# Token order of the key tiles, values in four loads, and scores by pairs of heads at the start of a fused attention and feed-forward kernel

## The chip, the cores and the metric

The kernel runs on one core of a Trainium2 chip. The metric is the device time of one execution in microseconds. Six parts of the core matter here: PE multiplies matrices, ACT evaluates functions, DVE and POOL work on vectors, SP issues stores, and 16 DMA engines move data. Loads that also convert from 32-bit to 16-bit floats are issued by POOL.

## The reference

```python
# q, k, v: (8, 12, 448, 64); w_in (768, 2048); w_out (2048, 768); beta (2048)
scores = q @ k.T / sqrt(64) - log(448)          # per batch and head
x = sigmoid(scores) @ v                         # 12 heads side by side: (8 * 448, 768)
h = x @ w_in
g = h * sigmoid(beta * h)
out = g @ w_out                                 # (3584, 768), float32
```

The sum over keys runs over all 448 of them, so the order in which keys stand inside a tile is free as long as k and v have the same one.

## The kernel before, in words

All matrix work is in 16-bit floats with sums in 32 bits. Everything is written in one order by hand (`tc.manual_schedule()`), and each engine does its instructions in that order; waits come only from data and from buffers.

**Heads and groups.** Four heads make a group (`g`, 24 in all, 3 for each batch), and two heads of a group make a slot. `load_one` (line 122) loads q or k of a group so that a partition holds one of 32 blocks of 14 tokens of one head (four heads times 32). `transpose` (line 201) turns blocks of 32 x 32 on DVE and leaves q and k with the head dimension on partitions: a head has 32 partitions, and its 64 dimensions are two passes (`e`). For k it needs two DVE instructions: one for the three full key tiles of 128 tokens (L217), one for the last 64 tokens (L221).

**Key tiles and values.** The 14 tokens of a block are numbered c. Before, quarter i of the 128 partitions of key tile j holds token c = 3i + j, and the last, half-filled tile holds c = 12 and 13. `load_v_full` (line 143) loads the values of the full tiles in four DMAs, `load_v_last` (line 155) those of the last tile in two. `double_v_last` (line 168) copies the last tile's 64 partitions to the other 64, on DVE, since two slots share one score tile there.

**Scores and weights.** `score` (line 231) issues one matmul (L237) that uses 32 of the 128 rows of the array. In the first batch the 448 queries are done in two halves of 224: `half_visit(g, c0, second)` (line 300) takes key tiles 0 and 1 of both slots (`second` = 0) or tile 2 and the last (`second` = 1), fills two score tiles with 16 matmuls that go through all four heads in turn, and then calls `weigh` (line 248) for each tile: one ACT sigmoid from PSUM to `attns` (L250, 896 or 448 columns). When only two score tiles are left, one sigmoid does both (L265, 1792 columns). `attend` (line 322) multiplies by the values (L340), and DVE casts the result to `xT` (L349). Score tiles are pairs of PSUM banks that are used in turn: three at first, two after the entry `("two",)`.

**First dense layer.** `dense1` (line 355) multiplies `xT` by `w_in` (L362), six matmuls for a block of 128 hidden columns; a sigmoid on ACT (L374) and a product on DVE (L377) give `gt`. In the first batch blocks 0 to 7 are done for the first half of the queries as soon as it is there. A "dense" unit in the list is one such matmul. Later the second layer (L392, L651) follows, largely by Strassen's scheme, and stores go out through SP.

**Order of the start.** `LOADS` (line 784) is the order of POOL's first DMAs after two that SP issues (k of group 0, and the first half of its q): q and k of groups 1 and 2, values of batch 0, the other halves of q, then eight loads of `w_in` with two blocks of 128 columns each. `LATER` (line 789) follows: group 3, `w_out`, the values of batch 1, and so on. `BEGIN` (line 838) is the order of the compute up to the first regular visit: casts, transposes, scores, idle matmuls on a tile of zeros (L822), values, dense units. In it `("q", 1, 0)` stands ahead of `("k", 1)`.

**Afterwards** each visit computes the scores of one key tile of a group, and a pace (`MORE`, line 900, moves single units between visits; `LATE` delays values) fills dense units between visits. There are 74 visits. From batch 1 on `load_v` loads a whole batch, and `double_v_last` copies it at a fixed visit.

Of the kernel before, what the change touches and what calls it, by code (L numbers as in the profile page):

```python
# [13 lines left out]
def kernel(  # L14
# [10 lines left out]
    nc = tc.nc  # L25
# [10 lines left out]
    PAIR = D // BLK  # L36
    JF = S // P
    KL = S - JF * P
    NF = JF * P // BLK
    NPAIR = H // 2  # L40
    QPB = H // HQ
    NHC = DM // P
# [97 lines left out]
    def last_base(s: int) -> int:  # L140
        return (s % 2 ^ swapped(s // 2)) * KL

    def load_v_full(b: int, lo: int = 0, hi: int = H):

        if b not in vs:
            vs[b] = vp.tile([P, H, JF + 1, D], FP16, tag="v16", name="v16")
        rows = v[b, lo:hi].rearrange("h (p c) d -> p h (c d)", c=NB)
        for i in range(HQ):
            nc.gpsimd.dma_start(
                out=vs[b][i * BLK : (i + 1) * BLK, lo:hi, 0:JF].rearrange("p h j d -> p h (j d)"),  # L150
                in_=rows[:, :, JF * i * D : JF * (i + 1) * D],
            )
            ready.update((b, "full", t, i) for t in range(lo // HQ, hi // HQ))

    def load_v_last(b: int):
        if b not in vs:
            vs[b] = vp.tile([P, H, JF + 1, D], FP16, tag="v16", name="v16")
        rows = v[b].rearrange("h (p c) d -> p h c d", c=NB)
        for c in range(NF, NB):
            lo = (c - NF) * BLK  # L160
            nc.gpsimd.dma_start(out=vs[b][lo : lo + BLK, :, JF], in_=rows[:, :, c])
        ready.add((b, "last"))

    def load_v(b: int):
        load_v_full(b)
        load_v_last(b)

    def double_v_last(b: int):
        assert (b, "last") in ready
        ready.add((b, "v"))  # L170
        nc.vector.tensor_copy(out=vs[b][KL:P, :, JF], in_=vs[b][0:KL, :, JF])

    WOUT = 2

# [26 lines left out]
    def transpose(g: int, r: int, c0: int = 0, c1: int = NB):  # L201
        raw = raws[g][:, r]
        assert g or (r, c0) == (0, NB // 2) or all((r, "cast", c) in ready for c in range(c0, c1))
        if r == 0:
            if g not in qT:
                qT[g] = qTp.tile([P, NB * BLK, PAIR], FP16, tag="qT", name="qT")
            ready.update((g, "q", c) for c in range(c0, c1, NB // 2))
            nc.vector.transpose(
                out=in_order(g // QPB, qT[g][:, c0 * BLK : c1 * BLK]),
                in_=raw[:, c0:c1].rearrange("p c d -> p (c d)").bitcast(FP32),  # L210
            )
            return
# [4 lines left out]
        nc.vector.transpose(  # L217
            out=to[:, 0 : JF * P].rearrange("p (j i q) -> p i j q", j=JF, i=HQ),
            in_=frm[:, 0:NF].rearrange("p (i j) f -> p i j f", j=JF),
        )  # L220
        nc.vector.transpose(  # L221
            out=to[:, JF * P :], in_=frm[:, NF:].rearrange("p c f -> p (c f)")
        )

    def score_tile():
        i, j = scored[n_sc[0] % len(scored)]
# [73 lines left out]
    def half_visit(g: int, c0: int, second: int):  # L300
# [18 lines left out]
        for s, jt, sco, u0 in plan:  # L319
            at_use(ats[id(sco)], (s, jt, c0), slice(u0, u0 + QH))  # L320

    def attend(g: int, c0: int, n: int, part=(0, 1)):
# [3 lines left out]
        assert (b, "v") in ready and (b, "full", t, HQ - 1) in ready  # L326
# [438 lines left out]
    with tc.manual_schedule():  # L765
        def load(what, *a):
            if what == "q":
                load_one(a[0], 0, a[1] * NH, (a[1] + 1) * NH)
            elif what == "k":
                load_one(a[0], 1)  # L770
            elif what == "qk":
                load_qk(a[0])
            elif what == "v":
                load_v_full(0, a[0] * HQ, a[1] * HQ)
            elif what == "last":
                load_v_last(0)
# [12 lines left out]
        LATER = [  # L789
# [42 lines left out]
        def beta_columns():  # L832
# [16 lines left out]
        for what, *a in BEGIN:  # L849
            if what == "q":  # L850
# [1 line left out]
                transpose(g, 0, half * NH, (half + 1) * NH)  # L852
            elif what == "k":
                transpose(a[0], 1)
            elif what == "scores":
                half_visit(a[0], a[1] * QH, a[2])
            elif what == "cast":
                cast(*a)
            elif what == "idle":
                idle_units(a[0])  # L860
            elif what == "v":
                double_v_last(a[0])
# [32 lines left out]
        def left_us(n: int):  # L895
# [2 lines left out]
        AV_US = 1.5  # L898
        GLANCE = 3
        MORE = {  # L900
# [3 lines left out]
        }  # L904
        RESERVE = (1.99, 3.28)
        LATE = {
# [122 lines left out]
```

## Time and profile before

| what | value |
|---|---|
| runs shown | 373.19, 373.23, 375.86 us; median 373.23 |
| profiled execution | 374.6 us, its span 372.8 us |
| PE busy | 365.8 us (98%), 2906 matmuls |
| DVE, ACT, POOL busy | 254.5, 259.9, 90.6 us |
| granted PE clock | 1.00 |
| matmuls L651 and L531 | 27% and 26% of the chain that ended last |
| sigmoid of 896 columns (L250), mean of one between 4 and 31 us | 1008 ns |
| issue of a value load, of a w_in load on POOL | 615 ns, 871 ns |

A line of the timeline has the start in us, the busy time of the merged instructions, the engine, the line of the code, what it writes and reads, the size, and how many; in brackets stands the engine's idle time before it and what ended that. A line of the stages has the stretch, its length, and for each engine the busy time and the number of instructions, then the granted PE clock, the DMA engines' share (over 1 where packets overlap) and their rate.

### The profile page before, as it was taken

The page shows a single profiled execution, that of the slowest core. Times are in us where ns is not written, and L with a number is a line of the kernel's source. Part 1 is how long each engine was busy: PE and PEld are TensorE (multiplying, and loading weights), DVE is VectorE, ACT ScalarE, POOL GpSimd, SP SyncE. Part 2 cuts the span into 40 slices and gives each one's busy share as a digit, 9 for nine tenths or more (in the row PEclk, how much of TensorE's full clock was granted, in tenths as well). Part 3 has the DMA queues.
Part 4 walks back from the last instruction along what each step waited for, and adds up shares of the span by engine and source line. Part 5 has one row for each costly group of instructions (what it writes and reads, how often), then busy time and mean ns, then how long its engine had stood idle before and what let it go on. Part 6 is the DMA issues. An engine that isn't in the chain of part 4 may idle for free.

```text
span 372.8 us, 7320 instructions
## 1 busy us (share of the span) xinstructions
PE 365.8 (98%) x2906; PEld 184.4 (49%) x2906; DVE 254.5 (68%) x479; ACT 259.9 (70%) x311; POOL 90.6 (24%) x136
## 2 busy tenths in 40 slices
PE   7989999999999999999999999999999999999997
PEld 4566644443444455544444445554444455555655
DVE  3435696877496966787667666778667666669671
ACT  5995777699876658887777749887787647883000
POOL 6833253151151012325123003235100002230000
PEclk9999999999999999999999999999999999999999
DMA  9999999993359030039829511018903111000334
GB/s 162 165 189 202 197 203 201 245 125 51 49 76 183 2 86 1 0 51 125 157 42 206 108 26 33 3 17 116 172 6 86 42 44 42 1 2 1 86 84 128
DMA packets 42626, 34.65 MB, mean 93 GB/s; under 512 B 21968, under 2 KB 39008, under 8 KB 42592
## 3 DMA queue, kind: packets, MB, share of 16 engines
q0 software_dynamic: 36688, 22.47, 44.5%
q1 hardware_dynamic: 5904, 11.71, 11.1%
q8 instruction: 23, 0.38, 0.4%
q14 instruction: 11, 0.09, 0.1%
HBM read 45.62 MB, written 11.01 MB: 152 GB/s over the span
## 4 chain that ended last, share of the span: by engine, by line
PE 92%; ACT 5%; issue 1%; DMA 1%; DVE 1%; ACTq 0%
PE ps L651 27%; PE ps L531 26%; PE ps L237 11%; PE ps L340 10%; PE ps L362 9%; PE ps L392 4%; PE ps L445 4%; ACT attns L250 3%; DMA gt<-in_k_dram 1%; ACT attns L265 1%; ACT sg L374 1%; DVE gt L377 0%; DVE kT L217 0%; ACT raw L806 0%; ACT osb L672 0%
## 5 line engine op out<-in xcount | busy, mean ns | idle before, releaser
L265 ACT ACTIVATE attns<-ps,nlogs 128x1792 f16<-128x1792 f32 x75 | 131.6, 1755 | 41.7 <-PE ps L237 41.6
L651 PEld LDWEIGHTS <-sum 128*128 128x128 f16 x440 | 40.5, 98 | 37.3 <-issue 12.5
L545 POOL TENSOR_TENSOR gt<-attns,sg 128x448 f16<-128x448 f32 x21 | 23.9, 1139 | 141.7 <-ACT sg L542 141.7
L237 PE MATMUL ps<-qT,kT 32*128 32x448 f16 (+3 forms) x864 | 52.1, 339 | 1.2 <-ACT attns L250 0.4
L542 ACT ACTIVATE sg<-ps,beta_sb 128x448 f32<-128x448 f32 x72 | 45.2, 632 | 8.4 <-PE ps L531 5.9
L531 PE MATMUL ps<-xT,w_in 128*128 128x448 f16 x216 | 49.2, 353 | 0.0
L531 PE MATMUL ps<-xT,w_S 128*128 128x448 f16 x216 | 49.2, 352 | 0.0
L651 PE MATMUL ps<-w_T,sum 128*128 128x384 f16 x264 | 48.7, 327 | 0.0
L545 DVE TENSOR_TENSOR gt<-ps,sg 128x448 f16<-128x448 f32 x72 | 44.3, 618 | 4.0 <-ACT sg L542 3.8
L349 DVE CAST xT<-ps 128x448 f16<-128x448 f32 (+1 forms) x54 | 28.8, 567 | 21.0 <-PE ps L340 21.0
L531 PEld LDWEIGHTS <-w_in 128*128 128x128 f16 x288 | 28.0, 98 | 26.6 <-issue 0.7
L362 PE MATMUL ps<-xT,w_in 128*128 128x448 f16 (+1 forms) x240 | 39.9, 316 | 1.2 <-DMA w_in<-in_moe_w_in_dram 0.6
L340 PE MATMUL ps<-attns,v 128*64 128x448 f16 (+3 forms) x432 | 40.4, 340 | 0.6 <-issue 0.6
L669 DVE TENSOR_TENSOR osb<-ps,osb 128x384 f32<-128x384 f32 x55 | 30.5, 554 | 15.1 <-PE ps L651 12.8
L638 DVE TENSOR_TENSOR sum<-gt 128x1024 f16<-128x1024 f16 x55 | 36.5, 678 | 0.2
L377 DVE TENSOR_TENSOR gt<-ps,sg 128x448 f16<-128x448 f32 (+1 forms) x40 | 20.1, 527 | 23.2 <-ACT sg L374 23.1
L126 POOL DMA_DIRECT2D raw<-in_q_dram x26 | 14.5, 559 | 79.6 <-DVE kT L221 72.6
L651 PE MATMUL ps<-w_out,gt 128*128 128x384 f16 x176 | 33.3, 327 | 0.0
L651 PE MATMUL ps<-w_out,sum 128*128 128x384 f16 x176 | 32.3, 327 | 0.0
L591 DVE TENSOR_TENSOR ps<-ps,attns 128x448 f32<-128x448 f32 x24 | 15.2, 632 | 23.3 <-PE ps L531 19.3
L362 PEld LDWEIGHTS <-w_in 128*128 128x128 f16 x240 | 21.8, 98 | 18.0 <-issue 5.4
L531 PEld LDWEIGHTS <-w_S 128*128 128x128 f16 x216 | 21.1, 98 | 19.4
(54 smaller groups left out, 376.4 us busy)
## 6 DMA issues: line engine op xcount, KB each, us to landing
out_dram<-osb SPq DMA_DIRECT2D x100, 96.0 KB, 2.1
raw<-in_k_dram POOLq DMA_DIRECT2D x23, 224.0 KB, 5.5
raw<-in_q_dram POOLq DMA_DIRECT2D x21, 224.0 KB, 3.9
v<-in_v_dram POOLq DMA_DIRECT2D x32, 144.0 KB, 6.2
w_in<-in_moe_w_in_dram POOLq DMA_DIRECT2D x8, 384.0 KB, 11.8
w_out<-in_moe_w_out_dram POOLq DMA_DIRECT2D x4, 768.0 KB, 13.4
v<-in_v_dram POOLq DMA_DIRECT2D x16, 48.0 KB, 6.1
out_dram<-osb SPq DMA_DIRECT2D x5, 144.0 KB, 2.4
```

Of the source, the lines that this page charges most:

```text
L237: nc.tensor.matmul(sco[base : base + nk, hh, u0 : u0 + n], kT[g][lo : lo + BLK, jt * P : jt * P + nk, e], qT[g][lo : lo + BLK, c0 : c0 + n ...
L265: nc.scalar.activation(out=attns[:, slot : slot + 2].rearrange("p n h s -> p (n h) s"), in_=sco, func=AF.Sigmoid, bias=nlogs[:, 0:1], scal ...
L340: nc.tensor.matmul(av[hh * D : (hh + 1) * D, 0:n], vs[b][base : base + nk, 2 * (s % NPAIR) + hh, jt], at[base : base + nk, hh, 0:n], start ...
L349: nc.vector.tensor_copy(out=xTs[b][:, s % NPAIR, c0 : c0 + n], in_=av[:, 0:n])
L362: nc.tensor.matmul(m1, w_in16[:, hc, dc * P : (dc + 1) * P], xTs[b][:, hc, c0 : c0 + n], start=(hc == 0), stop=(hc == NHC - 1),)
L377: nc.vector.tensor_tensor(out=gt[:, dc, off : off + n], in0=m1, in1=sg[:, 0:n], op=ALU.mult)
L531: nc.tensor.matmul(out, w[:, c, i * P : (i + 1) * P], m[:, c], start=(start and c == 0), stop=(c == KH - 1), skip_group_check=not start,)
L542: nc.scalar.activation(out=sg, in_=h, func=AF.Sigmoid, bias=0.0, scale=beta_sb[:, dc : dc + 1])
L545: return lambda: engine.tensor_tensor(out=gt[:, dc, b % 2 * S : b % 2 * S + S], in0=h, in1=sg, op=ALU.mult)
L638: nc.vector.tensor_tensor(out=sums[t, i], in0=x, in1=y, op=op)
L651: nc.tensor.matmul(m2, (x if op is None else sums[t, i])[:, dc], w[:, dc], start=first, stop=(dc == ND - 1), skip_group_check=i >= 4,)
L669: nc.vector.tensor_tensor(out=out, in0=in0, in1=in1, op=op)
```

## The change

Five things change; the arithmetic does not.

1. Token order: quarter i of the partitions now holds 4, 4, 3, 3 consecutive tokens (`rows_of`: first token 0, 4, 8, 11), the jth of them in key tile j. So the last tile's tokens are 3 and 7, and come with the others. The values of a batch are four DMAs with runs of 4 or 3 tokens of one head. In batch 0 they are loaded in two parts: heads 0 to 3 (group 0) first, heads 4 to 11 later, with four DMAs each.
2. The two DVE transposes of k are now halves of 256 and 192 columns (quarters 0 and 1, quarters 2 and 3) in place of 384 and 64.
3. The copy of the last value tile is done for batch 0 in the same two parts.
4. `pair_visit` replaces the half visits with `second` = 0 while three score tiles are in use: it takes one slot, that is two heads, and both key tiles 0 and 1, into one score tile with 8 matmuls, and its sigmoid follows.
5. Other orders: group 1's k ahead of its q, and group 0's values ahead of group 2's q, in the loads; group 0's values between group 1's scores in `BEGIN`; 29 idle matmuls for 42; 18 and 12 dense units around the scores of group 2 for 21 and 9, 33 for 39 before the third group's transposes; `MORE` changes at visits 2 and 3 by one unit each, and names 80 and 82 too.

```diff
+    def rows_of(i: int):
+        n = JF + int(i < KL // BLK)
+        return i * JF + min(i, KL // BLK), n
...
+    def load_v(b: int, lo: int = 0, hi: int = H):
...
         for i in range(HQ):
+            c, n = rows_of(i)
             nc.gpsimd.dma_start(
-                out=vs[b][i * BLK : (i + 1) * BLK, lo:hi, 0:JF].rearrange("p h j d -> p h (j d)"),
-                in_=rows[:, :, JF * i * D : JF * (i + 1) * D],
+                out=vs[b][i * BLK : (i + 1) * BLK, lo:hi, 0:n].rearrange("p h j d -> p h (j d)"),
+                in_=rows[:, :, c * D : (c + n) * D],
             )
...
+    def double_v_last(b: int, lo: int = 0, hi: int = QPB):
...
+        heads = slice(lo * HQ, hi * HQ)
+        nc.vector.tensor_copy(out=vs[b][KL:P, heads, JF], in_=vs[b][0:KL, heads, JF])
...
+        half = to.rearrange("p (x i q) -> p x i q", i=2, q=BLK)
+        for i in (0, 2):
+            c, n = rows_of(i)
+            nc.vector.transpose(
+                out=half[:, i // 2 :: 2].rearrange("p j i q -> p i j q"),
+                in_=frm[:, c : c + 2 * n].rearrange("p (i j) f -> p i j f", j=n),
+            )
...
+    def pair_visit(g: int, c0: int, x: int):
+        s, sco = 2 * g + x, score_tile()
+        for jt in (0, 1):
+            for e in range(PAIR):
+                for hh in range(2):
+                    score(sco, jt * QH, s, jt, hh, e, c0, QH)
+        slot = weigh(sco, S)
...
-            ("q", 1, 0), ("k", 1), ("k", 2), ("last",), ("q", 2, 0), ("v", 0, 3), ("q", 1, 1), ("q", 0, 1),
-            ("q", 2, 1), ("w_in", 0, 2), ("w_in", 2, 4), ("w_in", 4, 6), ("w_in", 6, 8), ("w_in", 8, 10),
+            ("k", 1), ("q", 1, 0), ("k", 2), ("v", 0, 1), ("q", 2, 0), ("v", 1, 3), ("q", 0, 1), ("q", 2, 1),
+            ("q", 1, 1), ("w_in", 0, 2), ("w_in", 2, 4), ("w_in", 4, 6), ("w_in", 6, 8), ("w_in", 8, 10),
...
-            ("q", 1, 0), ("idle", 20), ("scores", 0, 0, 1), ("idle", 4), ("scores", 0, 0, 0), ("k", 1),
-            ("idle", 2), ("k", 2), ("q", 2, 0), ("idle", 2), ("scores", 1, 0, 0), ("beta",), ("idle", 8),
-            ("scores", 1, 0, 1), ("v", 0), ("idle", 6), ("scores", 2, 0, 0), ("values", 0, 0), ("q", 1, 1),
-            ("scores", 2, 0, 1), ("q", 0, 1), ("values", 1, 0), ("scores", 0, 1, 0),
-            ("values", 2, 0), ("scores", 0, 1, 1), ("dense", 12), ("scores", 1, 1, 1), ("two",), ("dense", 6),
-            ("scores", 1, 1, 0), ("loads",), ("q", 2, 1), ("dense", 21), ("scores", 2, 1, 0), ("dense", 9),
-            ("values", 0, 1), ("scores", 2, 1, 1), ("values", 1, 1), ("values", 2, 1), ("dense", 39), ("k", 3),
-            ("q", 3, 0), ("q", 3, 1), ("dense", 45),
+            ("q", 1, 0), ("idle", 20), ("pair", 0, 0, 0), ("scores", 0, 0, 1), ("idle", 4), ("pair", 0, 0, 1),
+            ("k", 1), ("idle", 2), ("k", 2), ("v", 0, 1), ("pair", 1, 0, 1), ("q", 2, 0), ("pair", 1, 0, 0),
+            ("idle", 1), ("values", 0, 0), ("beta",), ("scores", 1, 0, 1), ("idle", 2), ("pair", 2, 0, 0),
+            ("pair", 2, 0, 1), ("v", 1, 3), ("q", 0, 1), ("q", 1, 1), ("values", 1, 0), ("scores", 2, 0, 1),
+            ("pair", 0, 1, 0), ("pair", 0, 1, 1), ("values", 2, 0), ("scores", 0, 1, 1), ("dense", 12),
+            ("scores", 1, 1, 1), ("two",), ("dense", 6), ("scores", 1, 1, 0), ("loads",), ("q", 2, 1),
+            ("dense", 18), ("scores", 2, 1, 0), ("dense", 12), ("values", 0, 1), ("scores", 2, 1, 1),
+            ("values", 1, 1), ("values", 2, 1), ("dense", 33), ("k", 3), ("q", 3, 1), ("q", 3, 0),
+            ("dense", 45),
```

More of the change, by code (lines that the diff above doesn't have):

```diff
@@ L38 @@
     KL = S - JF * P
-    NF = JF * P // BLK
     NPAIR = H // 2
@@ L148, in load_v_full @@
         for i in range(HQ):
+            c, n = rows_of(i)
             nc.gpsimd.dma_start(
-                out=vs[b][i * BLK : (i + 1) * BLK, lo:hi, 0:JF].rearrange("p h j d -> p h (j d)"),
-                in_=rows[:, :, JF * i * D : JF * (i + 1) * D],
+                out=vs[b][i * BLK : (i + 1) * BLK, lo:hi, 0:n].rearrange("p h j d -> p h (j d)"),
+                in_=rows[:, :, c * D : (c + n) * D],
             )
             ready.update((b, "full", t, i) for t in range(lo // HQ, hi // HQ))
[L155 to L171, printed above, removed]
+    def double_v_last(b: int, lo: int = 0, hi: int = QPB):
+        assert all((b, "full", t, i) in ready for t in range(lo, hi) for i in range(KL // BLK))
+        ready.update((b, "v", t) for t in range(lo, hi))
+        heads = slice(lo * HQ, hi * HQ)
+        nc.vector.tensor_copy(out=vs[b][KL:P, heads, JF], in_=vs[b][0:KL, heads, JF])
     WOUT = 2
@@ L320, in half_visit @@
             at_use(ats[id(sco)], (s, jt, c0), slice(u0, u0 + QH))
+    def pair_visit(g: int, c0: int, x: int):
[5 more added lines that the diff above has]
+        slot = weigh(sco, S)
+        for jt in (0, 1):
+            at_use(slot, (s, jt, c0), slice(jt * QH, (jt + 1) * QH))
     def attend(g: int, c0: int, n: int, part=(0, 1)):
@@ L325, in attend @@
             xTs[b] = xTp.tile([P, NHC, S], FP16, tag="xT", name="xT")
-        assert (b, "v") in ready and (b, "full", t, HQ - 1) in ready
+        assert (b, "v", t) in ready and (b, "full", t, HQ - 1) in ready
         slots = [2 * g + x for x in part]
@@ L773, in load @@
             elif what == "v":
-                load_v_full(0, a[0] * HQ, a[1] * HQ)
-            elif what == "last":
-                load_v_last(0)
+                load_v(0, a[0] * HQ, a[1] * HQ)
             elif what == "values":
@@ L854 @@
                 transpose(a[0], 1)
+            elif what == "pair":
+                pair_visit(a[0], a[1] * QH, a[2])
             elif what == "scores":
@@ L861 @@
             elif what == "v":
-                double_v_last(a[0])
+                double_v_last(0, *a)
             elif what == "values":
```

8 lines of the change are left out of this document (removed), and 4 rows, old and new, of the table MORE.

## The prediction

> **What bounds the kernel now.** I read the page first, then the busy times by stage, then who waits for whom on PE, then the timelines of PE and of POOL in the first 31 us.
>
> ```profile
> span 372.8 us, 7320 instructions
> PE 365.8 (98%) x2906; PEld 184.4 (49%) x2906; DVE 254.5 (68%) x479; ACT 259.9 (70%) x311; POOL 90.6 (24%) x136
> PE 92%; ACT 5%; issue 1%; DMA 1%; DVE 1%; ACTq 0%
> ```
>
> PE is the bound: 98% busy and 92% of the chain that ended last. Only time in which PE has nothing useful to do can be won, so the next view asks where that time lies.
>
> ```profile
> core 0: us, PE busy (x) PEld busy (x) DVE busy (x) ACT busy (x) POOL busy (x), PEclk, DMA share, GB/s
> 6.00:12.00 6.00, 5.40 (x83) 2.91 (x83) 2.51 (x9) 5.25 (x7) 3.12 (x7) 1.00 1.46 180
> 12.00:19.00 7.00, 6.29 (x118) 3.66 (x115) 3.47 (x11) 6.52 (x8) 6.43 (x8) 1.00 1.24 154
> 19.00:24.00 5.00, 4.04 (x60) 2.81 (x56) 1.46 (x5) 5.00 (x9) 1.10 (x2) 1.00 1.41 188
> 31.00:50.00 19.00, 19.00 (x146) 11.53 (x145) 12.47 (x26) 12.33 (x19) 7.49 (x12) 1.00 1.35 201
> ```
>
> From 31 us on PE is full (19.00 of 19.00), and the list of PE's waits has no entry of 0.3 us or more after 25 us. The diff leaves the matmuls behind that point the same in kind and number; it only shifts a few dense units between the next score visits. So the case is decided before 31 us. There ACT is nearly full from 6 to 24 us (5.25 of 6, 6.52 of 7, 5.00 of 5), and the DMA engines are full too (154 to 201 GB/s).
>
> ```profile
> 19.02 1.32 PE L362 MATMUL ps<-xT,w_in 128*128 128x224 f16 x12
> 20.28 0.70 PE L237 MATMUL ps<-qT,kT 32*128 32x224 f16 x16
> 21.56 0.73 PE L362 MATMUL ps<-xT,w_in 128*128 128x224 f16 x6 [0.58 <-DVE gt L377]
> 22.23 0.72 PE L237 MATMUL ps<-qT,kT 32*128 32x224 f16 x16
> 22.88 0.75 PE L362 MATMUL ps<-xT,w_in 128*128 128x224 f16 x6
> 24.24 1.81 PE L362 MATMUL ps<-xT,w_in 128*128 128x224 f16 x15 [0.62 <-DMA w_in<-in_moe_w_in_dram]
> 25.99 0.58 PE L237 MATMUL ps<-qT,kT 32*128 32x224 f16 x16
> ```
>
> At 24.24 PE stands still 0.62 us for the third load of w_in, whatever ACT did before. Its next 15 dense matmuls take 1.81 us, where 12 took 1.32: at (1.32 - 0.26)/11 = 0.096 us a step 15 need 1.60, so some 0.2 us more are lost within them, at the fourth load. Before 24 us a gain of ACT or PE is eaten by this wait; behind it PE is full. The arrival of w_in is the hinge.
>
> ```profile
> 8.56 0.61 POOL L149 DMA_DIRECT2D v<-in_v_dram  x1 [1.19 <-DMA raw<-in_k_dram]
> 9.80 0.56 POOL L126 DMA_DIRECT2D raw<-in_q_dram  x1 [0.63 <-DMA raw<-in_k_dram]
> 10.78 1.07 POOL L126 DMA_DIRECT2D raw<-in_q_dram  x2 [0.42 <-DMA v<-in_v_dram]
> 11.84 6.59 POOL L177 DMA_DIRECT2D w_in<-in_moe_w_in_dram  x8
> 21.27 0.54 POOL L126 DMA_DIRECT2D raw<-in_k_dram  x1 [1.22 <-DMA w_in<-in_moe_w_in_dram]
> 24.48 0.89 POOL L185 DMA_DIRECT2D w_out<-in_moe_w_out_dram  x1 [2.67 <-DMA w_in<-in_moe_w_in_dram]
> 25.83 0.88 POOL L185 DMA_DIRECT2D w_out<-in_moe_w_out_dram  x1 [0.46 <-DMA w_in<-in_moe_w_in_dram]
> 27.83 0.62 POOL L149 DMA_DIRECT2D v<-in_v_dram  x1 [1.11 <-DMA w_in<-in_moe_w_in_dram]
> ```
>
> Counted through, POOL's nth issue waits until the (n-8)th has landed: eight are in flight at most. The third w_in releases PE at 24.24 and POOL at 24.48, so a landing lies about 0.25 us ahead of the POOL row that it releases. Landings are then: group 1's k 8.3, group 2's k 9.55, first of the last value tile 10.5, w_in loads one to four at about 18.9 (PE's start at 19.02), 21.0, 24.2, 25.6, and then one each 2.0 us. The third is 1.2 us late against that pace.
>
> **The change, part by part.**
>
> *Value loads.* Before there are four of 144 KB and two of 48 KB; now there are four, for batch 0 twice four (heads 0 to 3, then 4 to 11). The bytes are the same. Written runs were 384 B and 128 B; they become 512 B and 384 B. DMA rates: 190 GB/s from 42.2 to 44 us (almost all 384 B), 199 from 22 to 24 (512 B), 194 from 44.5 to 46 (a mix with 128 B, of 1002 packets). So 672 KB of values take 3.5 us at 190 and 3.4 at 199: a gain of 0.1 to 0.3 us per batch, the upper end from the two last-tile loads, whose 96 KB took 9.55 to about 10.8 with their stragglers. I take 0.2. In batches 1 to 7 it buys nothing, since PE waits there for no value load; POOL saves two issues of 0.61 us a batch, of 24% busy.
>
> [...]
>
> *Order of the loads.* POOL has 13 issues ahead of w_in before and 15 after (7 of q and k, and 6, then 8, of values). By the rule of eight, the first w_in went out at 11.84, 0.5 us after the issue before it; two more of 0.61 us put it at 12.6 to 13.0. The loads ahead of it end 0.2 us earlier, at about 15.5 for 15.75. Whether the later issue delays the data depends on the time from issue to first byte, which no row gives for a full queue. Bounds for the arrival of w_in: -0.2 us (queue still full when it is issued) and +0.8 (the delay passes on one to one; +1.2 with both issues whole). 12.8 us is well ahead of 15.5, so I take -0.2 for the first load; the engines that drain early lose some of it, so for the third and fourth load -0.2 to +0.2, middle 0.
>
> *k ahead of q in the loads, q ahead of k on DVE.* DVE transposes group 1's q before its k. Before, q landed first (DVE at 6.50, then k at 8.30). Now q is the second to land, when both loads' bytes are through, at 8.3; k's transposes wait behind it: 8.3 + 0.41 + 0.78 = 9.45 instead of 9.0. Group 1's scores start 0.4 us later on PE. ACT has group 0 until 9.8 (below), so this costs ACT 0.1.
>
> *Key transposes.* 384 + 64 columns become 256 + 192. Rows: 384 takes 578 ns, 64 takes 203, 224 (L208) 370 to 411. By the line through the first two (1.17 ns a column) 256 + 192 is 428 + 353 = 781 ns, the same sum. Bounds 0.4 (twice the 64 row) to 1.16 (twice the 384 row) a group; even the upper one adds 0.38 x 24 = 9 us to a DVE that is idle 118 us, and it lies on the path only for group 1 (+0.4 at worst).
>
> *Doubling of the last value tile.* One copy of 0.42 us becomes two for batch 0, of 256 and 512 columns: 0.2 + 0.3, bounds 0.34 (twice the 0.17 of the smallest DVE row) to 0.84. The first waits for group 0's values, with q of group 2 and the first xT casts behind it on DVE; the second waits for values 1 to 3 at about 13.7, with two q transposes (of loads that land 14 to 15.5) and the next xT casts behind. The casts were at 16.65 before; 15.5 + 0.4 + 0.4 is earlier than that.
>
> *Scores by pairs.* A half visit did 16 matmuls with four heads in turn and filled two tiles together; a pair visit fills one tile with 8, two heads in turn: 3 steps of 0.096 + 0.26 = 0.55 us for a tile, where the first pair of tiles took 0.70 (5.94, x16). The first ACT op starts 0.15 earlier (6.55). PE's price is two times 0.4 for 0.5, +0.3 us a group, under ACT's 2 x 0.9 us (4.62 us for five on the chain). Group 0 ends on ACT at 6.55 + 3 x 0.9 + 0.53 = 9.8 for 10.1.
>
> *Group 0's values between group 1's scores.* Values 0 to 3 are 224 KB, as much as one k load (1.25 us): 9.55 + 1.25 = 10.8, up to 11.3 with the straggling seen at 10.5; + 0.2 for the copy. PE then does the 16 value matmuls (0.99) and only then the second half of group 1's scores. ACT has run dry at 11.7 (9.9 + 2 x 0.9) and resumes at 12.5 to 13.0: a new wait of 0.8 to 1.3 us. Gone in exchange are the stalls of before: PE's 0.57 at 14.08, with the 0.37 that ACT then waits at 15.75, and the 0.1 between its runs. ACT reaches the end of the six first visits between 20.0 and 21.0 (20.75 before). Cover: w_in. PE reaches the third load at 23.3 to 23.9, still ahead of 24.2.
>
> *13 fewer idle matmuls* (42 to 29, 0.11 us each): PE waits there for ACT anyway; 0 on time.
>
> *Dense 18, scores, dense 12* for 21, scores, 9: the 18 need three w_in loads only, so the 0.2 us at the fourth goes under the scores (0.58 us). The rest of the moved units (33 for 39, then +2 in MORE) only change places on a full PE; MORE's entries 80 and 82 name no visit, as there are 74.
>
> **Sum.** Third load 0, fourth load's gap -0.2; with it L265 for group 2 starts 0.5 us earlier, and its two sigmoids and gt free the banks for the last 32 value matmuls at 28.6 instead of 29.19, when PE gets there. I count -0.5 in all (between -0.2 and -0.6). The profiled execution took 374.6 us outside and 372.8 in its span; 372.3 in span, and against the median 373.23 of three runs: 372.7.
>
> **The rivals.**
>
> 1. *w_in late (slower).* Two more issues ahead, in a queue of eight: w_in leaves POOL at 12.8 and arrives 0.8 later. PE then waits at about 25.0 for the third load: +0.8 - 0.2 = +0.6, 373.8. It decides from an arrival 0.2 us later. For it: the DMA share falls to 1.24 in 12 to 19 us, so the queue was not full even before. Against: 15.5 is behind 12.8.
> 2. *The third load on time.* Its 1.2 us delay belongs to where other traffic falls, not to the program. At a pace of 2.0 it lands at 23.0 and PE's own work decides: start at 23.4 instead of 24.24, -0.8, and with the fourth load's -0.2 to -0.5 about 372.0. The same end is reached if short runs cost more than the rows at 190 GB/s show and all loads come 0.8 earlier. Against: no row shows a reason for either.
> 3. *Hidden anyway:* w_in +0.2 eats the 0.2 at the fourth load: 373.2.
> 4. *PE's clock.* PE stands idle for up to 1.2 us twice between 8 and 12 with fewer idle matmuls to fill it. If PE slows to half for one stretch of 3 us in which it is half busy, +1.5: 374.7. Against: the granted clock is 1.00 in every stage, and ACT is the limit there. [...]
>
> **How the numbers follow.** Forecast 0.40 (372.7); w_in late 0.18; third load on time 0.20; hidden 0.14; clock 0.05; something unseen in the full stretch 0.03. The range takes in rivals 1 to 3 with 0.4 for the bounds: 371.6 to 374.2, with the clock and the rest outside. One per cent is 3.7 us, about what a measurement can tell; no case reaches it but the unseen and the ends: faster 0.03, within 0.93, slower 0.04.
>
> **What would show it.** Right: no PE wait for values at 14; a new ACT wait for PE near 12; group 1's k transposes after 9; the first w_in issue near 12.8 but its use before 19.3; no lost time ahead of the dense 12; PE full from about 30.7. Wrong: PE's w_in wait moving by more than 0.4 us either way, matmul steps of twice 0.096 before 19 us, or any PE wait after 31.

## The result, and the profile after

| | median | lowest to highest | executions |
|---|---|---|---|
| kernel before | 373.31 us | 372.83 to 376.43 | 22 |
| changed kernel | 374.39 us | 373.56 to 377.77 | 22 |

The ratio is estimated at 1.0043, with the interval [1.0027, 1.0058]: slower, within one per cent. It weighs all executions and so lies above the ratio of the two medians (1.0029); the ratios further down are of the same kind. Two executions of the study that took 605.6 and 917.55 us are left out of every median and ratio. The forecast was 372.7 us with a range of 371.6 to 374.2; the median lies 0.2 us above the range and on the other side of no change. The profiled execution took 374.1 us, its span 372.3 us, at a granted clock of 1.00.

One list decided the study: the 22 executions with the mean granted clock of each. Twelve ran at a clock of 1.000 and took 373.56 to 374.46 us (median 373.79). Nine ran at 0.986 to 0.991 and took 375.89 to 377.77 (median 377.04); one, at 0.999, took 374.86. Of the kernel before, 94 executions in the experiments below, the one of 605.6 us (0.56) not among them, have their clock on record, and all lie at 0.999 or 1.000. So there are two results. At full clock the change costs 373.79 - 373.31 = 0.5 us, where 0.5 were forecast as a gain; and in about four executions of ten something else costs 2 to 4 us more, which lifts the median of all by another 0.6. The profiled execution is one of the first kind and shows nothing of the second. First the page of it:

```profile
span 372.3 us, 7277 instructions
PE 364.1 (98%) x2893; PEld 183.5 (49%) x2893; DVE 254.4 (68%) x480; ACT 259.5 (70%) x311; POOL 82.7 (22%) x124
PE 82%; DMA 13%; POOL 2%; ACT 2%; issue 1%; ACTq 0%; POOLq 0%
```

PE is as busy as before (98%), with 13 matmuls fewer. What changed is the third line: DMA has 13% of the chain that ended last, where it had 1%. In this execution the chain runs through transfers. The busy times by stage (columns as in the prediction) say where:

```profile
core 0: us, PE busy (x) PEld busy (x) DVE busy (x) ACT busy (x) POOL busy (x), PEclk, DMA share, GB/s
6.00:12.00 6.00, 4.56 (x81) 2.54 (x75) 3.01 (x10) 5.25 (x7) 3.96 (x8) 1.00 1.25 169
12.00:19.00 7.00, 6.01 (x102) 3.49 (x102) 3.10 (x12) 6.73 (x9) 6.66 (x9) 1.00 1.22 154
19.00:24.00 5.00, 4.42 (x64) 3.28 (x62) 1.44 (x4) 5.00 (x8) 1.58 (x3) 1.00 1.37 181
31.00:50.00 19.00, 19.00 (x146) 11.42 (x147) 12.79 (x26) 13.32 (x19) 6.25 (x10) 1.00 1.30 204
```

From 31 us PE is full, as forecast. From 12 to 19 us the DMA engines move 154 GB/s, the same as in the execution that the prediction worked from; an experiment will show that this isn't usual for the kernel before. PE's timeline:

```profile
10.30 0.99 PE L345 MATMUL ps<-attns,v 128*64 128x224 f16 x16 [0.58 <-DMA v<-in_v_dram]
...
13.90 0.99 PE L345 MATMUL ps<-attns,v 128*64 128x224 f16 x16 [0.29 <-DMA v<-in_v_dram]
...
18.69 1.32 PE L367 MATMUL ps<-xT,w_in 128*128 128x224 f16 x12
...
22.54 1.96 PE L367 MATMUL ps<-xT,w_in 128*128 128x224 f16 x18
...
25.37 1.32 PE L367 MATMUL ps<-xT,w_in 128*128 128x224 f16 x12 [0.24 <-DMA w_in<-in_moe_w_in_dram]
...
30.32 0.93 PE L367 MATMUL ps<-xT,w_in 128*128 128x448 f16 x4
...
59.39 0.65 PE L397 MATMUL ps<-w_out,gt 128*128 128x384 f16 x3 [0.23 <-DMA w_out<-in_moe_w_out_dram]
```

PE waits for values of both parts (10.30 and 13.90), for a load of w_in (25.37), and at 59.39, where the prediction saw a PE without waits, for the last load of w_out. POOL's timeline shows why these loads are late:

```profile
7.28 0.60 POOL L154 DMA_DIRECT2D v<-in_v_dram  x1 [1.50 <-DMA raw<-in_k_dram]
8.11 0.58 POOL L154 DMA_DIRECT2D v<-in_v_dram  x1 [0.24 <-DMA raw<-in_q_dram]
9.21 1.14 POOL L154 DMA_DIRECT2D v<-in_v_dram  x2 [0.52 <-DMA raw<-in_k_dram]
10.35 1.65 POOL L125 DMA_DIRECT2D raw<-in_q_dram  x3
11.95 6.61 POOL L171 DMA_DIRECT2D w_in<-in_moe_w_in_dram  x8
```

POOL waits for earlier loads to land (the brackets), up to 9.21; from there on it waits for nothing, issues two loads of values and three of q in a row, and reaches w_in at 11.95.

### The profile page after: what moved, and what is told of

The parts are those of the page before. It is cut to its first block, busy times and chain, and to the rows that moved or that the text cites. A ratio compares the mean times of both kernels' runs of the same rounds, so it can differ in the third digit from the quotient of the medians.

```text
span 372.3 us, 7277 instructions
## 1 busy us (share of the span) xinstructions
PE 364.1 (98%) x2893; PEld 183.5 (49%) x2893; DVE 254.4 (68%) x480; ACT 259.5 (70%) x311; POOL 82.7 (22%) x124
## 4 chain that ended last, share of the span: by engine, by line
PE 82%; DMA 13%; POOL 2%; ACT 2%; issue 1%; ACTq 0%; POOLq 0%
PE ps L656 27%; PE ps L536 26%; PE ps L231 9%; PE ps L345 8%; PE ps L367 5%; DMA v<-in_v_dram 5%; PE ps L450 4%; DMA w_out<-in_moe_w_out_dram 4%; DMA w_in<-in_moe_w_in_dram 3%; PE ps L397 2%; DMA raw<-in_k_dram 2%; ACT attns L259 1%; POOL w_in L171 1%; POOL raw L125 1%; POOL v L154 0%
```

## The experiments

Two theories stand against each other. *Loads late*: eight value loads in place of six put w_in, and all that is behind it, later, and the DMA engines run dry. *PE's clock*: the idle matmuls that went kept the clock up, and without them it falls to half for some microseconds. A third, that the new order of the compute itself is at fault, is kept as a rival. Times are medians of executions, with lowest and highest and their number, beside those of the kernel before on the same chip (medians of 373.45 to 373.49).

**The kernel before, once more.** No edit.

> The kernel before, once more, for a second profile of it. Theory A (the profiled execution of before, 374.6 us, was 1.3 us above its median because its third w_in load came 1.2 us late; a usual execution does not have that wait): time 373.2 to 373.5, and a profile with 371.4 to 371.8 us of span whose wait of PE for w_in near 24 us is under 0.2 us. Theory B (the wait for the third w_in load is always there, and the 1.3 us lie outside the program's span): the same median, but a span near 372.8 with 0.6 us of wait at 24 us.

373.56 us (372.92 to 374.30, 11 executions), ratio 0.9998 [0.9986, 1.0011], span 371.3. Its stages and PE's timeline:

```profile
core 0: us, PE busy (x) PEld busy (x) DVE busy (x) ACT busy (x) POOL busy (x), PEclk, DMA share, GB/s
9.83:13.24 3.41, 3.22 (x46) 1.78 (x44) 1.61 (x6) 3.38 (x5) 3.41 (x6) 1.00 1.46 193
...
12.00:19.00 7.00, 6.85 (x123) 4.22 (x121) 2.68 (x8) 6.90 (x9) 5.90 (x8) 1.00 1.35 183
```

```profile
18.34 1.32 PE L362 MATMUL ps<-xT,w_in 128*128 128x224 f16 x12
...
22.19 2.19 PE L362 MATMUL ps<-xT,w_in 128*128 128x224 f16 x21
...
29.63 1.69 PE L362 MATMUL ps<-xT,w_in 128*128 128x448 f16 x8
```

```profile
10.73 6.60 POOL L177 DMA_DIRECT2D w_in<-in_moe_w_in_dram  x8
```

No bracket: in this execution, whose time is near the median, PE waits for no load of w_in. The 21 dense matmuls follow on without the 0.62 us that the prediction saw at 24.24, the DMA engines move 183 GB/s from 12 to 19 us and not 154, and the first load of w_in is issued at 10.73 and not 11.84, and lands at 16.92. The execution behind the prediction had a span of 372.8, 1.5 us above this one. Beside this one, not that one, the changed kernel starts its dense stretch at 30.32 for 29.63: 0.7 us late. With the wait at 59.39 that is 0.9 of the 1.0 us by which the spans differ. (By their times, 374.1 and 373.12, the two profiled executions lie 0.3 above and 0.4 below the medians of their kinds, so the 1.0 here stands for 0.5 between the medians.)

**The changed kernel, once more.** No edit.

> The changed kernel once more, for a second profile and more times. Theory A (DMA stream: the last load of w_out lands at 59.3 us and PE waits for it, so what the start wins is eaten there): 373.6 to 374.5 us, ratio 1.001 to 1.005 to before, and again a wait of PE for w_out near 58.8 us. Theory C (the median differs only because more executions of the changed kernel ran at a granted clock under 1): with executions at full clock alone the two kernels agree within 0.2 us.

377.49 us (376.82 to 377.66, 4 executions), ratio 1.0103 [1.009, 1.0116], all at a clock of 0.982 to 0.986: the second kind of execution, now with a profile. Its stages, cut where the granted clock changes, and PE's timeline:

```profile
11.02:14.43 3.41, 2.19 (x40) 1.11 (x37) 1.69 (x7) 2.86 (x5) 3.41 (x6) 1.00 1.19 150
14.43:24.67 10.24, 9.99 (x104) 5.53 (x108) 2.67 (x8) 6.34 (x9) 5.93 (x8) 0.50 1.36 177
24.67:31.00 6.33, 6.00 (x88) 4.57 (x84) 2.10 (x6) 6.00 (x8) 2.12 (x3) 1.00 1.45 198
```

```profile
14.42 1.66 PE L345 MATMUL ps<-attns,v 128*64 128x224 f16 x16 [0.99 <-DMA v<-in_v_dram]
...
21.66 2.42 PE L367 MATMUL ps<-xT,w_in 128*128 128x224 f16 x12
```

The first row is the 3.41 us ahead of the fall: PE works 2.19 of them, 64%, and its longest wait is the 0.99 for values. Then the granted clock is 0.50 for 10.24 us, three times 3.41, and 1.00 again behind it. The same 16 value matmuls take 1.66 us for 0.99, the same 12 dense ones 2.42 for 1.32. The span is 375.6, 3.3 above that of the profiled full-clock execution. None of the four ran at full clock, so what was expected of such executions could not be looked at here; PE's list of waits has none for w_out.

**Token order and four loads, without the split; order and 42 idle matmuls of before.**

```diff
-            ("q", 1, 0), ("k", 1), ("k", 2), ("last",), ("q", 2, 0), ("v", 0, 3), ("q", 1, 1), ("q", 0, 1),
+            ("q", 1, 0), ("k", 1), ("k", 2), ("q", 2, 0), ("v", 0, 3), ("q", 1, 1), ("q", 0, 1),
```

> One part alone: token order of the key tiles, values in four loads (for batch 0 too, all heads at once, where the four full loads were), halves in the key transposes. Loads and compute otherwise in the order of before, with half visits. Theory A (DMA stream): two issues fewer ahead of w_in and 0.2 to 0.3 us less DMA time, so w_in and w_out land 0.2 to 0.6 us earlier and the time is 0 to 0.5 us under before. Rival (the new layout itself costs, by slower transposes or uneven loads): 0.5 us or more above before.

373.53 us (372.93 to 374.76, 12), ratio 1.0001 [0.9993, 1.001]. The new token order, the longer runs and the other split of the key transposes are worth nothing that can be measured. The expected gain did not come although w_in was issued earlier (10.18 for 10.73) and the DMA engines moved 198 GB/s from 12 to 19 us. One execution, of 374.76, has a clock of 0.995.

**The loads of the change, the compute order of before.**

```diff
+            ("k", 1), ("q", 1, 0), ("k", 2), ("v", 0, 1), ("q", 2, 0), ("v", 1, 3), ("q", 0, 1), ("q", 2, 1),
+            ("q", 1, 1), ("w_in", 0, 2), ("w_in", 2, 4), ("w_in", 4, 6), ("w_in", 6, 8), ("w_in", 8, 10),
...
+            ("scores", 1, 0, 1), ("v", 0, 1), ("v", 1, 3), ("idle", 6), ("scores", 2, 0, 0), ("values", 0, 0), ("q", 1, 1),
```

> Token order and load order of the changed kernel (values of batch 0 in two parts, group 0's first), compute order of before (half visits, group 0's values after group 2's first scores, 42 idle matmuls, 21 and 9 and 39 dense units). Theory A (the loads decide, by when the last w_out load lands): as the changed kernel, 373.6 to 374.5. Rival D (the compute order costs: the new wait of ACT near 11.5 us and the later scores): 0.4 us or more under the changed kernel, about the time of before.

375.07 us (374.11 to 375.89, 6), ratio 1.0042 [1.0028, 1.0056]; five of six at a clock of 1.0. This is above the expected 373.6 to 374.5. It puts a loss of 1.6 us on the side of the loads, but it isn't clean: the second half of group 1's q is now loaded last and still transposed first, and PE waits 1.65 us for it at 17.68. In the profiled execution the clock is half behind that wait:

```profile
16.38:19.78 3.40, 2.10 (x45) 1.30 (x48) 1.85 (x6) 1.80 (x3) 2.14 (x4) 1.00 1.24 155
19.78:23.19 3.41, 3.41 (x36) 1.94 (x32) 0.66 (x3) 2.73 (x5) 0.81 (x3) 0.50 1.43 189
```

So the split of the values had to be tried alone (below).

**The changed kernel with 46 idle matmuls.**

```diff
-            ("k", 1), ("idle", 2), ("k", 2), ("v", 0, 1), ("pair", 1, 0, 1), ("q", 2, 0), ("pair", 1, 0, 0),
-            ("idle", 1), ("values", 0, 0), ("beta",), ("scores", 1, 0, 1), ("idle", 2), ("pair", 2, 0, 0),
-            ("pair", 2, 0, 1), ("v", 1, 3), ("q", 0, 1), ("q", 1, 1), ("values", 1, 0), ("scores", 2, 0, 1),
+            ("k", 1), ("idle", 8), ("k", 2), ("v", 0, 1), ("pair", 1, 0, 1), ("q", 2, 0), ("pair", 1, 0, 0),
+            ("idle", 6), ("values", 0, 0), ("beta",), ("scores", 1, 0, 1), ("idle", 2), ("pair", 2, 0, 0),
+            ("pair", 2, 0, 1), ("v", 1, 3), ("q", 0, 1), ("q", 1, 1), ("idle", 6), ("values", 1, 0), ("scores", 2, 0, 1),
```

> The changed kernel with 46 idle matmuls instead of 29: 8 for 2 ahead of group 1's first pair, 6 for 1 ahead of group 0's values, and 6 new ones ahead of group 1's values, each where PE waited 0.5 to 1.0 us. Theory C (PE's granted clock falls to half for 3.4 us or a multiple after a stretch in which PE did too little; the changed kernel's long executions are those): no execution with a clock under 0.999, times 373.5 to 374.5, all in the lower group of the changed kernel. Rival A (only late loads make the change slower, and the low clock comes from outside the program): still about half of the executions at 0.986 to 0.991 and 375 to 377.7 us.

374.26 us (373.71 to 377.63, 12), ratio 1.0031 [1.001, 1.0051]. One execution of 12 has a clock of 0.991 (377.03), the others 0.999 or more, where the changed kernel had 13 of 26 at or below 0.991 (nine of 22, four of four). The fill takes most of the second kind away and not all, where none was expected to be left; one of 377.63 at a clock of 0.999 stays unexplained. Without these two the median is 374.2, for 373.5. What is left would fit the late loads, since PE still waits 0.48 us for values at 14.91, but it is not shown: the long dense stretch starts at 31.01 here, 0.7 later than in the profiled execution of the changed kernel, so the fill may itself cost time.

**The changed kernel with the second half of group 2's q behind three loads of w_in.**

```diff
-            ("k", 1), ("q", 1, 0), ("k", 2), ("v", 0, 1), ("q", 2, 0), ("v", 1, 3), ("q", 0, 1), ("q", 2, 1),
-            ("q", 1, 1), ("w_in", 0, 2), ("w_in", 2, 4), ("w_in", 4, 6), ("w_in", 6, 8), ("w_in", 8, 10),
+            ("k", 1), ("q", 1, 0), ("k", 2), ("v", 0, 1), ("q", 2, 0), ("v", 1, 3), ("q", 0, 1), ("q", 1, 1),
+            ("w_in", 0, 2), ("w_in", 2, 4), ("w_in", 4, 6), ("q", 2, 1), ("w_in", 6, 8), ("w_in", 8, 10),
```

> The changed kernel with the second half of group 2's q loaded behind the third w_in load instead of ahead of the first: 14 issues ahead of w_in for 15. Theory A (the first w_in load leaves POOL too late, the DMA engines run dry between 12 and 19 us at 154 to 159 GB/s where the usual execution of before has 183, and the stream, down to the last load of w_out, lands 1.4 us later): the first w_in is issued about 0.5 us earlier, the rate from 12 to 19 rises over 165 GB/s, w_out's last load lands 0.3 us or more earlier than 59.3 and executions at full clock take 0.2 to 0.5 us less than the changed kernel's 373.8. Rival (the stream has slack): no change of full-clock times within 0.2 us.

374.26 us (372.93 to 377.91, 11), ratio 1.004 [1.0011, 1.0069]. The expectation for the transfers was missed: the first issue of w_in moved only from 11.95 to 11.60, and the rate from 12 to 19 us stayed at 154 GB/s. Five of 11 executions lie at 0.986 to 0.991; of the profiled one the clock is 0.50 from 16.97 to 23.80 (6.83 us, twice 3.41), after 3.41 us in which PE worked 1.84:

```profile
12.00:15.41 3.41, 1.61 (x24) 0.92 (x22) 1.32 (x6) 3.28 (x4) 3.41 (x5) 1.00 1.17 144
13.56:16.97 3.41, 1.84 (x39) 1.02 (x37) 1.43 (x4) 1.90 (x3) 3.40 (x5) 1.00 1.21 147
16.97:23.80 6.83, 6.54 (x60) 3.76 (x60) 0.95 (x4) 5.20 (x7) 3.31 (x6) 0.50 1.35 178
```

The five at 1.000 took 372.93 to 374.26, too scattered to say that one load less ahead of w_in helps.

**The kernel before, with 29 idle matmuls and nothing else changed.**

```diff
-            ("idle", 2), ("k", 2), ("q", 2, 0), ("idle", 2), ("scores", 1, 0, 0), ("beta",), ("idle", 8),
-            ("scores", 1, 0, 1), ("v", 0), ("idle", 6), ("scores", 2, 0, 0), ("values", 0, 0), ("q", 1, 1),
+            ("idle", 2), ("k", 2), ("q", 2, 0), ("idle", 2), ("scores", 1, 0, 0), ("beta",), ("idle", 1),
+            ("scores", 1, 0, 1), ("v", 0), ("scores", 2, 0, 0), ("values", 0, 0), ("q", 1, 1),
```

> The kernel before with 29 idle matmuls, as in the changed kernel, instead of 42 (1 for 8 ahead of the second half of group 1's scores, none for 6 ahead of group 2's). Theory C1 (fewer idle matmuls alone bring the half clock): a part of the executions at a clock under 0.995, and these 2 us or more longer; the others as before, 373.0 to 374. Rival C2 (it takes the new waits of PE for values and keys; in before's order the idle matmuls only fill short waits): all executions at 0.999 or 1.000, ratio 1.000 within 0.001.

374.81 us (374.38 to 375.53, 9), ratio 1.0035 [1.0024, 1.0047], and all nine at a clock of 0.991 to 0.995. Stages, PE's timeline and PE's waits:

```profile
9.83:13.24 3.41, 1.84 (x37) 0.96 (x33) 1.77 (x8) 3.41 (x5) 3.41 (x6) 1.00 1.50 192
13.24:16.65 3.41, 3.41 (x50) 1.82 (x40) 1.26 (x4) 2.38 (x4) 3.41 (x5) 0.50 1.35 181
```

```profile
13.69 1.67 PE L340 MATMUL ps<-attns,v 128*64 128x224 f16 x16
16.29 1.14 PE L340 MATMUL ps<-attns,v 128*64 128x224 f16 x16
```

```profile
PE ps L237 <- ACT attns L250: 2.1, 5, 0.6
```

This is the clearest of the runs: the clock is under 0.999 in nine executions of nine, and in none of the 94 of the kernel before. The loads are those of before (192 GB/s), ACT is full (3.41 of 3.41), and PE does wait for ACT, as the prediction said of the idle matmuls: five times, 0.63 us at most. But PE works only 1.84 of the 3.41 us, where with its idle matmuls it worked 3.22 (the same stretch in the first experiment's stages), and then the clock is 0.50 for 3.41 us, and ACT in its turn goes without work (2.38). Thirteen matmuls that compute nothing are worth 1.3 us here.

**Token order and pairs, order and loads of before.** As the third experiment, and with this:

```diff
-            ("q", 1, 0), ("idle", 20), ("scores", 0, 0, 1), ("idle", 4), ("scores", 0, 0, 0), ("k", 1),
-            ("idle", 2), ("k", 2), ("q", 2, 0), ("idle", 2), ("scores", 1, 0, 0), ("beta",), ("idle", 8),
-            ("scores", 1, 0, 1), ("v", 0, 3), ("idle", 6), ("scores", 2, 0, 0), ("values", 0, 0), ("q", 1, 1),
+            ("q", 1, 0), ("idle", 20), ("scores", 0, 0, 1), ("idle", 4), ("pair", 0, 0, 0), ("pair", 0, 0, 1), ("k", 1),
+            ("idle", 2), ("k", 2), ("q", 2, 0), ("idle", 2), ("pair", 1, 0, 0), ("pair", 1, 0, 1), ("beta",), ("idle", 8),
+            ("scores", 1, 0, 1), ("v", 0, 3), ("idle", 6), ("pair", 2, 0, 0), ("pair", 2, 0, 1), ("values", 0, 0), ("q", 1, 1),
```

> Token order with values in four loads in the order of before (as in the run with the tokens alone, 373.53), and in addition pairs of heads instead of the half visits with key tiles 0 and 1, 42 idle matmuls in their places. If pairs win what they should (first sigmoid 0.15 us earlier, score tiles freed one by one), 0.1 to 0.5 us under 373.5. Rival (two heads in turn use half of the array's rows, PE needs 0.3 us more a group and ACT is the limit anyway): 373.5 to 374.

373.02 us (372.84 to 373.46, 12), ratio 0.9986 [0.9977, 0.9995], span 371.1, no clock under 0.999: faster than both kernels, by about 0.5 us beside the kernel before. Its stages, then POOL:

```profile
12.00:19.00 7.00, 6.62 (x123) 4.45 (x122) 2.79 (x9) 6.65 (x9) 5.43 (x7) 1.00 1.41 197
```

```profile
9.99 0.83 POOL L171 DMA_DIRECT2D w_in<-in_moe_w_in_dram  x1
```

With four value loads only 11 issues are ahead of w_in; it goes out at 9.99 and the DMA engines stay full (197 GB/s).

**The same with group 1's k loaded first,** and then with k first for DVE too.

```diff
-            ("q", 1, 0), ("k", 1), ("k", 2), ("q", 2, 0), ("v", 0, 3), ("q", 1, 1), ("q", 0, 1),
+            ("k", 1), ("q", 1, 0), ("k", 2), ("q", 2, 0), ("v", 0, 3), ("q", 1, 1), ("q", 0, 1),
```

> The best version so far (token order, values in four loads, pairs of heads in the order of before, 42 idle matmuls: 373.02 us) with one edit: group 1's k loaded ahead of its q, while DVE still transposes q first. Theory A: both transposes wait for the second load, so group 1's scores start 0.3 to 0.5 us later; ACT has work until then, so at full clock 0 to 0.3 us over 373.0. If the longer wait of PE near 8.5 us is enough for the half clock, some executions with a clock under 0.996 and 1 us or more longer.

373.00 us (372.59 to 373.56, 11), ratio 0.9985 [0.9977, 0.9994]. Loading k first costs nothing.

```diff
-            ("q", 1, 0), ("idle", 20), ("scores", 0, 0, 1), ("idle", 4), ("pair", 0, 0, 0), ("pair", 0, 0, 1), ("k", 1),
+            ("idle", 20), ("scores", 0, 0, 1), ("idle", 4), ("pair", 0, 0, 0), ("pair", 0, 0, 1), ("k", 1), ("q", 1, 0),
```

> As the run with group 1's k loaded first, and DVE transposes that k first too. Theory A (the cost of k first is DVE's order): the k transposes run 0.5 to 1 us earlier, hidden under the wait for q, and the time is that of the best version, 373.0, or up to 0.2 less. Rival (it costs by another way, such as the loads themselves): as with DVE's order unchanged.

373.01 us (372.63 to 374.49, 11), ratio 0.999 [0.9981, 0.9999]. No further gain. The slowest execution has a clock of 0.995.

**Token order and pairs, and the values of batch 0 in two parts: the split alone.** Group 0's values also move ahead of group 2's q, and DVE's copy of the last tile is done in the same two parts (not shown).

```diff
-            ("q", 1, 0), ("k", 1), ("k", 2), ("q", 2, 0), ("v", 0, 3), ("q", 1, 1), ("q", 0, 1),
+            ("q", 1, 0), ("k", 1), ("k", 2), ("v", 0, 1), ("q", 2, 0), ("v", 1, 3), ("q", 1, 1), ("q", 0, 1),
```

> The best version so far with one edit: the values of batch 0 in two parts of four loads, group 0's ahead of group 2's q, as in the changed kernel (15 issues ahead of w_in for 11), compute order of before. Theory A (the number of issues ahead of w_in decides when w_in leaves POOL and how dry the DMA engines run): first w_in issue at 11 to 12 us instead of 10.0, rate from 12 to 19 us under 175 GB/s instead of 197, w_out's last load at 58.5 or later instead of 57.7, time 0.3 to 1.2 us over 373.0. Rival (issues are free while the queue is full): w_in and the time as in the best version, within 0.2.

374.76 us (374.14 to 375.15, 5, all at a clock of 1.0), ratio 1.0031 [1.0019, 1.0043], span 373.4. That is 1.7 us above the kernel without the split, more than was expected. Stages, POOL, PE's waits and PE's timeline:

```profile
12.00:19.00 7.00, 6.37 (x118) 3.80 (x116) 3.33 (x11) 6.66 (x10) 6.91 (x9) 1.00 1.16 145
```

```profile
9.56 1.14 POOL L154 DMA_DIRECT2D v<-in_v_dram  x2 [0.69 <-DMA raw<-in_k_dram]
10.70 1.65 POOL L125 DMA_DIRECT2D raw<-in_q_dram  x3
12.31 6.60 POOL L171 DMA_DIRECT2D w_in<-in_moe_w_in_dram  x8
```

```profile
PE ps L367 <- DMA w_in<-in_moe_w_in_dram: 1.9, 3, 1.0
```

```profile
19.74 1.32 PE L367 MATMUL ps<-xT,w_in 128*128 128x224 f16 x12 [0.97 <-DMA w_in<-in_moe_w_in_dram]
```

The bytes are the same; only their number of DMAs grew from four to eight. The first w_in goes out 2.3 us later (12.31 for 9.99): that is the time of four more issues of 0.6 us on POOL, which waits for no landing from 9.56 on. From 12 to 19 us the engines move 145 GB/s for 197, and PE waits 1.9 us for w_in in three places. (197 - 145) x 7 us is 364 KB, about one load of w_in (384 KB), or 1.8 us at 197 GB/s: as much as the whole loss. The first issue of w_out, 24.14 for 21.23, and the landing of its last load, 60.48 for 57.67, show that the delay is carried along for 40 us.

**The changed kernel with the last load of w_out in two DMAs.**

```diff
-            ("w_out", 1, 1),
+            ("w_out_part", 8, 12, 1), ("w_out_part", 12, 16, 1),
```

> The changed kernel with the last load of w_out (eight blocks of rows, second half of the columns) in two of four blocks each. Theory A (at full clock the changed kernel loses 0.4 us at 58.8 us, where PE waits for that load, landing at 59.3): the first of the two lands about 2 us earlier, the wait goes, and executions at full clock take 373.2 to 373.5 instead of 373.6 to 374.0. Rival (PE's place there is free anyway): full-clock times unchanged. The half clock is untouched by the edit: a third to all of the executions below 0.996.

376.07 us (373.02 to 377.97, 12), ratio 1.0063 [1.0036, 1.009]. Eight of 12 executions have a clock of 0.986 to 0.991 and hide the question. The four at 0.999 or more took 373.02, 373.26, 373.98 and 374.42; the profiled one (374.42) has no wait for w_out, but PE gets there 0.8 us later. They are too few to settle it. What this run does show is how a clock of 0.986 to 0.991, at 375.86 to 377.97 us, drowns a gain of some tenths.

## Why the prediction was wrong

Two things cost time, and the runs part them. *PE's clock* is shown by the two runs of the idle matmuls: the kernel before gets the lower clock from losing 13 of them (nine of nine at 0.991 to 0.995; the profiled one has 0.50 for 3.41 us), and the changed kernel mostly loses it when it gets 17 (one of 12 at 0.991, for 13 of 26 at 0.982 to 0.991). With 42 it is rare and not gone (at 0.995, one of 12 in the third experiment, one of 11 with k first for DVE too, one of six with the loads alone). *Loads late* is shown by the split alone, at full clock, and by its rates. The third theory, the compute order, finds no support: the split costs 1.7 us at full clock and pairs with the token order gain 0.5, while the whole change costs 0.5 there; so the rest of it, group 0's values between group 1's scores above all, seems to give back 0.7 (worked out from the others as if they add up; that part was not run alone).

The median lies 1.7 us above the forecast of 372.7. 1.1 of that is there at full clock (373.79), where the loads and the base of the sum went wrong; 0.6 comes from the executions at a lower clock, and it is this part that takes the median out of the range. That the case is decided early was right: in all 14 profiles the span is the start of the long dense stretch near 30 us plus 341.5 to 342.0 us (29.63 and 371.3 in the kernel before, repeated; 30.32 and 372.3 in the changed kernel; 31.50 and 373.4 with the split alone; 34.03 and 375.6 at half clock).

Point by point:

- **The failed step: "13 fewer idle matmuls: PE waits there for ACT anyway; 0 on time."** They cost no time on PE, but the clock stayed up with them: in the kernel before 94 executions of 94 lie at 0.999 or 1.000 with 42, nine of nine at 0.991 to 0.995 with 29. With 29 of them 13 of 26 executions of the changed kernel had a mean clock of 0.982 to 0.991, at 2 to 4 us each; the one of them that was profiled had the clock at half for 10.24 us. The rival *PE's clock* named this loss, with a price of 1.5 (the runs: 1.3 in the kernel before, 2 to 4 in the changed one) and a chance of 0.05. No run shows its stretch of 3 us at half clock; the four profiles have 3.41 (twice), 6.83 and 10.24. In all four the 3.41 us ahead of the half clock had PE at work for 1.84 to 2.19 us, and the longest waits were 0.6 to 1.7 us. So a low share of work, without a longer wait, stood ahead of each fall, though such a share did not always bring one (last section). The granted clock of 1.00 in every stage, given as evidence against, was that of a kernel with the fill in it.
- **The second: "Order of the loads ... I take -0.2".** Beside the usual execution of the kernel before, the two more issues (0.61 us each) came whole: the first w_in is issued at 11.95 for 10.73, +1.2, and lands at 18.32 for 16.92, +1.4, above even the upper bound of 1.2. The -0.2 needed a queue that is still full when w_in is issued. The prediction called the DMA engines full at 154 to 201 GB/s, and 154 from 12 to 19 us is not full: two runs with fewer issues move 197 and 198 there. Whether the size of the value loads adds to it is not shown; no run parts that from the issue time.
- **The base of the sum.** The -0.5 was made of waits (0.62 and 0.2 for w_in) of one execution that took 374.6 us where the median was 373.23. The repeated profile doesn't have them: the execution behind the prediction already had its w_in late (issued at 11.84, landed at about 18.9, later than in the changed kernel). Against that execution the span fell by the 0.5 that was forecast (372.3 for 372.8), in part by luck: the long dense stretch starts 0.9 earlier (30.32 for 31.21), and 0.4 is lost behind it, where no loss was forecast. Against the median there was nothing to win. The prediction noted the difference of 1.4 us and subtracted from the median all the same.
- **The rival *w_in late*** (373.8) gave the time of the full-clock executions (373.79). It named the late w_in (issued at 11.95 for 10.73), but that the two agree so closely is luck: it added 0.6 to a base that was late already, and its place is only partly right, since PE waits 0.24 us at 25.37 and the rest is spread over values, ACT and the last w_out. The forecast of no wait behind 31 us failed there.
- **"Dense 18, scores, dense 12 ... -0.2" failed too,** as a result of the second point: the 18 run through (1.96 us at 22.54), but the load behind them is later, and the dense 12 wait 0.24 for it. The wait for values at 14, forecast to go, is down from 0.57 to 0.29 only, and the usual execution of the kernel before has none there.
- **Group 1's k transposes "after 9" failed as well:** they run from 8.19 on, since q had landed by 7.85 and not at 8.3 (and 8.3 + 0.41 + 0.78 is 9.49, not 9.45).
- **Confirmed:** a new ACT wait for PE near 12 (0.55 at 11.97, less than the 0.8 to 1.3 of the forecast); the transposes of k at 431 + 335 = 766 ns for a forecast of 781; the copies at 221 + 286 ns for 0.2 + 0.3; PE full from 31 to 50.

## What to carry to other kernels

Before idle matmuls, or any filler on PE, are taken out, add up PE's work over stretches of 3.41 us, the shortest half clock seen here, and compare executions by their granted clock; a kernel whose time falls into two heaps may have a clock that falls in one of them. Where one queue issues the loads in order, count the issues ahead of the load that matters: splitting a load to get its first part sooner put the loads behind it 0.6 us later for each part more (w_in at 12.31 for 9.99 with four more). And take a sum of waits only from an execution whose own time is that of the median, or repeat the profile.

## What was not expected of the hardware

The half clock came in stretches of 3.41 us (the kernel before with 29 idle matmuls, the loads alone), 6.83 (group 2's q later) and 10.24 (the changed kernel), one, two and three times 3.41, and without any idle stretch of that length: PE's longest waits ahead of them were 0.63, 1.65, 1.57 and 0.99 us. What sets these lengths is not shown.

A low share of work did not always bring the fall. The changed kernel has 64% ahead of the fall in one execution, and in the profiled one at full clock 61%, without a fall:

```profile
8.00:11.41 3.41, 2.09 (x43) 1.23 (x41) 2.27 (x8) 3.41 (x5) 2.77 (x5) 1.00 1.23 159
```

In the run with group 2's q later the clock was still 1.00 behind 3.41 us with 1.61 of work (47%, 12.00 to 15.41), and fell 1.6 us later. What sets the moment of a fall is not shown, and no threshold either. Nor do the runs part time at work from rows at work: an idle matmul uses 128 rows of the array, a score matmul 32 (`128*128` and `32*128` in the trace).

Nor does one long wait stand ahead of the fall in the kernel before with 29 idle matmuls: PE's waits for ACT, all ahead of it, are the five of 0.63 us at most, 2.1 in all.

Why the clock stayed at half for three times 3.41 us in one profile, while PE worked 9.99 of 10.24 us, is open.
